# A transposing DMA for the rows of the summed tanh gradient, and one transfer for the rows of F

## The chip, the cores and the metric

The kernel runs on one core of a Trainium2 chip. Its time is the device time of one execution in microseconds, the median of three runs. The profile is of one further execution, taken by the hardware profiler. The engines are TensorE (PE; its weight loads are PEld), VectorE (DVE), ScalarE (ACT), GpSimd (POOL) and SyncE (SP). Each works through its own queue in order. SP computes nothing here: it issues transfers (DMA), as POOL does beside its additions.

## The reference

The kernel computes a small speech model and its gradients. B = 2 sequences of T = 16000 rows with D = 256 features go through two convolutions of three taps, each followed by gelu and a step of 2; the 4000 rows that are left are joined with U = 8 vectors per sequence:

```python
h  = gelu(conv3(x, w1))[:, ::2]          # 8000 rows
f  = gelu(conv3(h, w2))[:, ::2]          # 4000 rows: F
fe = f @ w_f
ge = g @ w_g
j  = tanh(fe[:, :, None, :] + ge[:, None, :, :])
out = j @ w_o                            # (2, 4000, 8, 256)
```

With grad_out given for out, it returns out and the gradients of x, w1, w2, g, w_f, w_g and w_o. One of them matters here. The gradient at fe is the sum over u of (1 - j^2) * (grad_out @ w_o^T); the kernel keeps its negative, bf16, as NGFE. The gradient of w_f is then F^T times that, a product over the 4000 rows of each sequence. TensorE sums over the partitions, so both F and NGFE are needed with rows in the partitions, while the kernel produces both with features in the partitions. The two edits concern how these row forms, FR and NR, are made.

## The kernel before

The two sequences stand behind one another on an axis of 8016 columns, cut into G = 16 chunks of 512 (the last has 336). A tile holds features in the partitions and the columns of a chunk in the free dimension, in KT = 2 halves.

The outer loop runs over the chunks. Pass n has four parts, up = 0 to 3, each with two values of u. A part's main work is the joint of chunk n (joint_units, L670): the gradient of tanh (gj, L612: TensorE multiplies GOT with the transposed w_o at L623, DVE forms NGZ at L627), the sum over u on POOL (ngfe_acc, L632, whose last addition writes NGFE), the output (o_block, L685) and the gradient of w_o (gwo, L721, which reads JR, the rows of the tanh, and GO). weave (L742) alternates it with a fill: after each of the 12 units of main work the fill is due 0.92 units more.

The fill of pass n is the forward convolution of chunk n + 1 and the backward work of chunk n - 1, in a fixed order written at L832: two units of conv, one of d1, one of conv, the other of d1, the last of conv, then rows and d5 in alternation, then gwf, gw2, ghr, conv2 and e. d1 multiplies NGFE with the transposed w_f. row_units (L472) makes the rows: its first unit transposes NGFE by eight TensorE transposes against the identity into one PSUM buffer (L460) and copies it out by one DVE instruction (L462) into a tile of the pool "rows" (six buffers); four more units do the same for h and the gradient behind the second gelu. gwf_units (L499) multiplies FR and NR into the gradient of w_f (L506); it takes 8 matmuls.

The Python order is the order of the work where engines and their data allow it; the framework that builds the program may bring an instruction forward on its engine's queue where its inputs are due earlier, and adds the waits that the tiles need. Every transfer also waits for the one issued eight before it on the same queue kind.

SyncE's queue holds, per pass, eight GOT loads (transposing, L172), four GO loads (plain, L198), eight JR loads (transposing, from JT, L658), four XC loads (transposing, rows of x for chunk n + 2, L164) and the two halves of FR (load_fr, L464, transposing, from FT). JR has two buffers, so the load of one pair of u waits for the gwo matmuls (L729) that read the pair before the last. load_fr(n) stands at the beginning of part up == 1 of pass n; FR has one buffer, and its readers run in pass n + 1.

After the loop a tail does the backward work of chunk 15, and then writes the accumulated gradients; the small gradient of g and w_g uses two small tiles there, gg_sb and ngR.

Of the kernel before, what the change touches and what calls it, by code (L numbers as in the profile page):

```python
# [13 lines left out]
BF16 = mybir.dt.bfloat16  # L14
FP32 = mybir.dt.float32
ALU = mybir.AluOpType
ACT = mybir.ActivationFunctionType
# [5 lines left out]
P = 128  # L23
KT = 2
KK = 3
D = 256
V = 256
U = 8
CW = 512
# [3 lines left out]
def kernel(  # L33
# [22 lines left out]
    nc = tc.nc  # L56
# [7 lines left out]
    def geom(n):  # L64
        c0 = n * CW
        return c0, min(CW, L - c0)

    def segs(n, back=0):

        c0, W = geom(n)  # L70
        out = []
        for b, base in ((0, 0), (1, B1)):
            lo, hi = max(c0 - back, base), min(c0 + W, base + MQ)
            if hi > lo:
# [3 lines left out]
    def gaps(n, back=0):  # L78

        W = geom(n)[1]  # L80
        at, out = -back, []
        for b, q, col, w in segs(n, back):
            if col > at:
                out.append((at, col))
            at = col + w
        if W > at:
            out.append((at, W))
        return out

    def blocks(w):  # L90
        return [(o, min(P, w - o)) for o in range(0, w, P)]

    def nsets(n):
        return 4 if geom(n)[1] == CW else 3

    def sets(n):
        s = nsets(n)
        return [(k, geom(n)[1] // s) for k in range(s)]

    pool = lambda name, bufs, **kw: ctx.enter_context(tc.tile_pool(name=name, bufs=bufs, **kw))  # L100
# [8 lines left out]
    frp = pool("frp", 1)  # L109
    accp = pool("accp", 1)  # L110
    gfp = pool("gfp", 2)
    ghp = pool("ghp", 2)
    rowp = pool("rowp", 6)
    xrp = pool("xrp", 1)
    gxp = pool("gxp", 2)
    jtp = pool("jtp", 7)
# [10 lines left out]
    def ps_f32():  # L127
        return psp.tile([P, 512], FP32, name="ps", tag="ps")

    def ps_bf():  # L130
        return psp.tile([P, 8, P], BF16, name="pst", tag="ps")


    ident = const.tile([P, P], BF16, name="ident")
# [18 lines left out]
    S = [dict() for _ in range(G)]  # L153


    def load_x(n, phases=(0, 1, 3, 2)):
        W = geom(n)[1]
        for c in phases:
            t = xcp.tile([P, KT, CW + 16], BF16, name="XC")
            back = 16 if c == 3 else 0  # L160
            for lo, hi in gaps(n, back):
                nc.vector.memset(t[:, :, 16 + lo:16 + hi], 0.0)
            for b, q, col, w in segs(n, back):
                nc.sync.dma_start_transpose(out=t[:, :, 16 + col:16 + col + w], in_=xq[b, c, q:q + w, :])  # L164
            S[n]["X", c] = t
# [290 lines left out]
    def transposes(srcs, dsts, evict=None):  # L456

        ps = ps_bf()
        for src, j, M in srcs:
            nc.tensor.transpose(out=ps[:M, j, :], in_=src, identity=ident[:])  # L460
        for dst, M, j0, j1 in dsts:
            (evict or nc.vector.tensor_copy)(out=dst, in_=ps[:M, j0:j1, :])  # L462

    def load_fr(n):  # L464
        W = geom(n)[1]
        FR = frp.tile([P, KT, 4, P], BF16, name="FR")
        nb = len(blocks(W))
        for kt in range(KT):
            nc.sync.dma_start_transpose(out=FR[:, kt, 0:nb, :], in_=S[n]["FT"][:, kt, 0:nb * P])
        S[n]["FR"] = FR  # L470

    def row_units(n):  # L472
        c0, W = geom(n)
        st = S[n]
        HT, GF, FT, NG = st["HT"], st["GF"], st["FT"], st["NGFE"]
        bl = blocks(W)
        FR = st["FR"]
        t = rowp.tile([P, 8, P], BF16, name="rows")
        st["NR"] = t
        srcs = [(NG[:, kt, o:o + M], 2 * j + kt, M) for j, (o, M) in enumerate(bl) for kt in range(KT)]  # L480
        dsts = [(t[:M, 2 * j:2 * j + 2, :], M, 2 * j, 2 * j + 2) for j, (o, M) in enumerate(bl)]
        if W == CW:
            dsts = [(t[:], P, 0, 8)]
        transposes(srcs, dsts)
        yield
        st["HG"] = []
        s = nsets(n)
        for k, M in sets(n):
            t = rowp.tile([P, 8, P], BF16, name="rows")
            col = lambda off: slice(off + k, off + k + s * (M - 1) + 1, s)  # L490
            srcs = [(HT[:, par, kt, col(2)], 2 * par + kt, M) for par in range(2) for kt in range(KT)]
            srcs += [(GF[:, kt, col(2)], 4 + kt, M) for kt in range(KT)]
            if k == 0:
                srcs += [(HT[:, 1, kt, col(1)], 6 + kt, M) for kt in range(KT)]
            transposes(srcs, [(t[:M, 0:len(srcs)], M, 0, len(srcs))], nc.scalar.copy)
            st["HG"].append(t)
            yield

    def gwf_units(n):  # L499
        W = geom(n)[1]  # L500
        FR, t = S[n]["FR"], S[n]["NR"]
        bl = blocks(W)
        ps = ps_f32()
        for k, (o, M) in enumerate(bl):
            for dt in range(KT):
                nc.tensor.matmul(ps[:, dt * D:(dt + 1) * D], lhsT=FR[:M, dt, k, :],  # L506
                                 rhs=t[:M, 2 * k:2 * k + 2, :].rearrange("p k d -> p (k d)"),
                                 start=(k == 0 and dt == 0), stop=(k == len(bl) - 1 and dt == KT - 1))
        flush("F", ACCF[:], ps[:])
        first_flush["F"] = False  # L510
        yield
# [226 lines left out]
    def empty(k):  # L738
        for _ in range(k):
            yield  # L740
# [83 lines left out]
    for n in range(G):  # L824
        back, fwd = n > 0, n + 1 < G
        conv = conv_units(n + 1) if fwd else iter(())
        conv2 = conv2_units(n + 1) if fwd else iter(())
        late_open[0] = False
        parts = []
        if back:  # L830
            d1, e, rows, ghr = d1_units(n - 1), e_units(n - 1), row_units(n - 1), ghr_units(n - 1)
            parts += [islice(conv, 2), islice(d1, 1), islice(conv, 1), d1, conv, alternate(rows, d5_units(n - 1)),  # L832
                      gwf_units(n - 1), gw2_units(n - 1), islice(ghr, 1), islice(conv2, 1), ghr, conv2, islice(e, 6)]
            if fwd:
                parts.append(fe_units(n + 1))
            parts.append(e)
        else:
            parts += [conv, empty(3), islice(conv2, 1), empty(3), conv2, empty(3), fe_units(n + 1)]
        fill = chain(*parts)
        ratio = (0.92 if n > 0 else 0.4) if n + 1 < G else 0.72  # L840
        for up in range(U // 2):
            step = n * (U // 2) + up
            for i in range(2):
                if 2 * step + 4 + i < len(order):
                    load_got(*order[2 * step + 4 + i])
            if step + 1 < len(orderp):
                load_go(*orderp[step + 1])
            if up == 1:
                load_fr(n)
            if back and up < 2:  # L850
                load_xr(n - 1, 2 * up)
                load_xr(n - 1, 2 * up + 1)
            main = joint_units(n, up)
            weave(main, fill, ratio)
            if up == U // 2 - 1:
                for _ in fill:
                    pump(2)
                    pump_late(1)
                pump(len(later))
                late_open[0] = True  # L860
                pump_late(len(late))
            for i in range(2):
                if 2 * step + 2 + i < len(order):
                    tanh(*order[2 * step + 2 + i])
            if step + 1 < len(orderp):
                load_jr(*orderp[step + 1])
            if n + 2 < G:
                load_x(n + 2, ((0, 1, 3, 2)[up],))
    n = G - 1
# [9 lines left out]
    for i in range(KK):  # L879
# [15 lines left out]
                            in_=NGGEc[:].rearrange("p b k u c -> p (b k u) c"),  # L895
# [4 lines left out]
    for b in range(B):  # L900
        gg = ps_f32()
        for kt in range(KT):
            nc.tensor.matmul(gg[:U, 0:D], lhsT=NGGEb[:, b, kt, :], rhs=WGT[:, kt, :], start=(kt == 0), stop=(kt == KT - 1))
        gg_sb = gxp.tile([U, D], BF16, name="gg_sb")
        nc.scalar.activation(out=gg_sb[:], in_=gg[:U, 0:D], func=ACT.Copy, scale=-1.0)
        nc.sync.dma_start(out=out_4[b], in_=gg_sb[:])
        tr = ps_bf()
        for kt in range(KT):
            nc.tensor.transpose(out=tr[:U, kt, :], in_=NGGEb[:, b, kt, :], identity=ident[:])
        ngR = gxp.tile([U, KT, P], BF16, name="ngR")  # L910
        nc.vector.tensor_copy(out=ngR[:], in_=tr[:U, 0:KT, :])
        for dt in range(KT):
            nc.tensor.matmul(GWG_ps[:, dt * D:(dt + 1) * D], lhsT=GR8[:, b, dt * P:(dt + 1) * P],
                             rhs=ngR[:].rearrange("u kt p -> u (kt p)"),
                             start=(b == 0 and dt == 0), stop=(b == B - 1 and dt == KT - 1))
# [33 lines left out]
```

## Time and profile before

| what | value |
|---|---|
| median of 3 runs | 849.85 us (844.79 to 854.31) |
| profiled execution | 843.12 us, span 841.4 us |
| granted TensorE clock, mean | 0.994 |
| GOT loads | 136, 5.7 us to landing (median) |
| JR loads | 128, 4.8 us |
| XC loads | 68, 5.6 us |
| FR loads (halves) | 32, 5.6 us |
| mean rate of the transfers | 223 GB/s |

The span runs from the first instruction to the last. "To landing" runs from the start of the issuing instruction to the end of the transfer. In the rows of the profile a name such as `PE ps L524` is an engine, the tile that it writes and a line of the kernel; an arrow to the left in a wait names what ended it. SPq is SyncE's queue; the time of one of its instructions holds any wait in it, and the least that a transposing one takes is about 1.2 us.

### The profile page before, as it was taken

The page shows a single profiled execution, that of the slowest core. Times are in us where ns is not written, and L with a number is a line of the kernel's source. Part 1 is how long each engine was busy: PE and PEld are TensorE (multiplying, and loading weights), DVE is VectorE, ACT ScalarE, POOL GpSimd, SP SyncE. Part 2 cuts the span into 40 slices and gives each one's busy share as a digit, 9 for nine tenths or more (in the row PEclk, how much of TensorE's full clock was granted, in tenths as well). Part 3 has the DMA queues.
Part 4 walks back from the last instruction along what each step waited for, and adds up shares of the span by engine and source line. Part 5 has one row for each costly group of instructions (what it writes and reads, how often), then busy time and mean ns, then how long its engine had stood idle before and what let it go on. Part 6 is the DMA issues. An engine that isn't in the chain of part 4 may idle for free.

```text
span 841.4 us, 17055 instructions
## 1 busy us (share of the span) xinstructions
PE 812.8 (97%) x6396; PEld 598.2 (71%) x6396; DVE 620.3 (74%) x1217; ACT 678.4 (81%) x1080; POOL 394.6 (47%) x423
## 2 busy tenths in 40 slices
PE   7969999999999999999999999999999999999997
PEld 3546677767768677676766777677686776878796
DVE  4896696876778767697866968768687676967644
ACT  3889998796978969699796987969789696987744
POOL 1154544444534535444486644445345354445661
PEclk9999999999999999999999999999999999999999
DMA  9988999999999999999999999999999999999954
GB/s 188 194 198 182 212 229 233 216 251 235 225 221 259 226 229 245 243 222 183 224 255 210 233 233 228 251 210 265 238 237 264 210 227 231 220 210 228 243 157 135
DMA packets 398515, 187.21 MB, mean 223 GB/s; under 512 B 346464, under 2 KB 382200, under 8 KB 398432
## 3 DMA queue, kind: packets, MB, share of 16 engines
q1 hardware_dynamic: 378112, 119.00, 77.9%
q0 software_dynamic: 20320, 67.12, 27.5%
q8 instruction: 50, 0.82, 0.4%
q14 instruction: 33, 0.27, 0.1%
HBM read 51.38 MB, written 50.34 MB: 121 GB/s over the span
## 4 chain that ended last, share of the span: by engine, by line
PE 43%; ACT 41%; DVE 6%; issue 5%; DMA 4%; POOL 0%; SPq 0%; ACTq 0%; POOLq 0%; DVEq 0%
ACT JT L396 12%; PE ps L593 7%; ACT OUT L692 6%; ACT JSQ L617 6%; PE GWO_ps L729 6%; PE ps L580 6%; PE ps L690 6%; ACT rows L462 5%; PE ps L355 5%; PE ps L524 4%; PE ps L623 4%; ACT g_s L260 3%; ACT g_x L323 3%; PE pst L460 2%; ACT GX L583 2%
## 5 line engine op out<-in xcount | busy, mean ns | idle before, releaser
L646 POOL TENSOR_TENSOR ACCN<-ACCN,NGZ 128x1024 f32<-128x1024 f32 (+1 forms) x80 | 168.7, 2109 | 69.1 <-DVE NGZ L627 68.0
L627 DVE SCALAR_TENSOR_TENSOR NGZ<-JSQ,ps 128x512 bf16<-128x512 bf16 (+3 forms) x272 | 167.5, 640 | 43.2 <-PE ps L623 39.9
L692 ACT CAST OUT<-ps 128x512 bf16<-128x512 f32 (+1 forms) x252 | 148.4, 600 | 58.4 <-PE ps L690 58.2
L396 ACT ACTIVATE JT<-FE,GE 128x512 bf16<-128x512 f32 (+3 forms) x272 | 182.3, 711 | 4.0 <-PE ps L623 1.9
L617 ACT ACTIVATE JSQ<-JT 128x1024 bf16<-128x1024 bf16 (+1 forms) x128 | 135.8, 1064 | 25.6 <-DVE NGZ L627 25.6
L729 PE MATMUL GWO_ps<-GO,JR 128*128 128x256 bf16 (+1 forms) x1008 | 148.6, 273 | 2.1 <-DVE JR L462 2.1
L690 PE MATMUL ps<-WO,JT 128*128 128x256 bf16 (+1 forms) x1008 | 148.7, 274 | 0.3 <-ACT rows L462 0.3
L717 POOL DMA_DIRECT2D out_dram<-OUT x76 | 55.8, 735 | 184.4 <-ACT OUT L692 171.5
L623 PE MATMUL ps<-GOT,WOT 128*128 128x512 bf16 (+1 forms) x512 | 139.2, 376 | 0.8 <-DVE rows L462 0.8
L260 DVE SCALAR_TENSOR_TENSOR g_s<-g_sq,g_x 128x1024 bf16<-128x1024 bf16 (+2 forms) x49 | 81.2, 1657 | 50.1 <-ACT g_sq L260 50.1
L729 PEld LDWEIGHTS <-JR 128*128 128x128 bf16 (+1 forms) x1008 | 96.9, 98 | 28.6 <-DVE JR L462 2.4
L690 PEld LDWEIGHTS <-JT 128*128 128x128 bf16 (+1 forms) x1008 | 97.9, 98 | 22.1 <-issue 1.6
L580 PE MATMUL ps<-W1T,GH 128*128 128x256 bf16 (+2 forms) x756 | 100.4, 273 | 0.0
L408 DVE TENSOR_TENSOR ACC<-ACC,ps 128x512 f32<-128x512 f32 x90 | 61.5, 684 | 44.5 <-PE ps L524 32.8
L580 PEld LDWEIGHTS <-GH 128*128 128x128 bf16 (+2 forms) x756 | 83.5, 116 | 13.0
L320 PE MATMUL ps<-XC,W 128*128 128x512 bf16 (+1 forms) x384 | 91.3, 375 | 1.1 <-DMA XC<-in_x_dram 1.1
L593 PE MATMUL ps<-rows,XR 128*128 128x256 bf16 (+1 forms) x756 | 90.4, 273 | 0.0
L593 PEld LDWEIGHTS <-XR 128*128 128x128 bf16 (+1 forms) x756 | 74.0, 98 | 11.6
L583 ACT CAST GX<-ps 128x512 bf16<-128x512 f32 (+2 forms) x126 | 72.2, 587 | 10.5 <-DMA out_dram<-GX 4.1
L241 POOL DMA_DIRECT2D out_dram<-GX x67 | 36.7, 548 | 82.1 <-ACT GX L583 75.0
L623 PEld LDWEIGHTS <-WOT 128*128 128x128 bf16 x512 | 48.5, 98 | 33.6 <-issue 2.3
L320 PEld LDWEIGHTS <-W 128*128 128x128 bf16 x384 | 37.4, 98 | 38.5 <-issue 1.4
(131 smaller groups left out, 1214.2 us busy)
## 6 DMA issues: line engine op xcount, KB each, us to landing
GO<-in_grad_out_dram SPq DMA_DIRECT2D x56, 512.0 KB, 5.3
out_dram<-OUT POOLq DMA_DIRECT2D x56, 512.0 KB, 5.5
out_dram<-GX POOLq DMA_DIRECT2D x55, 256.0 KB, 4.3
XR<-in_x_dram POOLq DMA_DIRECT2D x39, 256.0 KB, 6.3
XR<-in_x_dram POOLq DMA_DIRECT2D x13, 320.0 KB, 6.2
GOT<-in_grad_out_dram SPq DMA_TRANSPOSE x136, 5.7
JR<-JT SPq DMA_TRANSPOSE x128, 4.8
GO<-in_grad_out_dram SPq DMA_DIRECT2D x4, 384.0 KB, 5.0
```

The lines of the kernel that those rows point to most:

```text
L260: later.popleft()()
L320: nc.tensor.matmul(ps[:, :W], lhsT=W1[:, i, kt, mt * P:(mt + 1) * P], rhs=st["X", c][:, kt, 16 + sh:16 + sh + W], start=(k == 0), stop=(k ...
L396: nc.scalar.activation(out=JT[:, mt, lo:hi], in_=S[n]["FE"][:, mt, lo:hi], func=ACT.Tanh, bias=GE[:, b, mt, u:u + 1], scale=1.0)
L580: nc.tensor.matmul(ps[:M, cj * D:(cj + 1) * D], lhsT=GH[:, par, kt, o:o + s * (M - 1) + 1:s], rhs=W1T[:, i, kt, :], start=(j == 0), stop=( ...
L593: nc.tensor.matmul(ps[:, dt * D:(dt + 1) * D], lhsT=XR[:M, 4 * k + i + 2 * (1 - par), dt * P:(dt + 1) * P], rhs=t[:M, g + 2 * par:g + 2 * ...
L617: nc.scalar.activation(out=JSQ[:, :, :W], in_=JT[:, :, :W], func=ACT.Square)
L623: nc.tensor.matmul(ps[:, :W], lhsT=WOT[:, kt, mt * P:(mt + 1) * P], rhs=GOT[:, kt, :W], start=(kt == 0), stop=(kt == KT - 1))
L627: nc.vector.scalar_tensor_tensor(out=NGZ[:, mt, lo:hi], in0=JSQ[:, mt, lo:hi], scalar=1.0, in1=ps[:, lo:hi], op0=ALU.subtract, op1=ALU.mul ...
L646: st["last"] = nc.gpsimd.tensor_tensor(out=out, in0=in0, in1=st["NGZ", u][:, :, :W], op=ALU.add)
L690: nc.tensor.matmul(ps[:M, j * V:(j + 1) * V], lhsT=st["JT", u][:, kt, o:o + M], rhs=WO[:, kt, :], start=(kt == 0), stop=(kt == KT - 1))
L692: nc.scalar.copy(out=OUT[:M, k, :], in_=ps[:M, :])
L729: nc.tensor.matmul(GWO_ps[:, dt, :], lhsT=JR[:M, j, dt, k, :], rhs=GO[:M, k, j * V:(j + 1) * V], start=(n_gwo[0] == 0), stop=(n_gwo[0] == ...
```

## The change

The rows of NGFE get a pool of their own, nrp, with one buffer, and a function load_nr that fills it by a transposing DMA. It is called at the beginning of part up == 1 for chunk n - 1, just ahead of load_fr. row_units makes the rows by TensorE, as before, if NR is not there when it begins; it then copies them in up to four instructions instead of one, as the tile's layout is now [partition, half, block, feature]. FR is loaded by one transfer instead of two for chunks of 512 columns. The two small tiles of the tail are taken from the pool "rows".

```diff
+    nrp = pool("nrp", 1)
...
+    def load_rows(pool_, name, src, W):
+        t = pool_.tile([P, KT, 4, P], BF16, name=name)
+        if W == CW:
+            nc.sync.dma_start_transpose(out=t[:].rearrange("p k a d -> p (k a) d"), in_=src.rearrange("p k w -> p (k w)"))
+        else:
+            nb = len(blocks(W))
+            for kt in range(KT):
+                nc.sync.dma_start_transpose(out=t[:, kt, 0:nb, :], in_=src[:, kt, 0:nb * P])
+        return t
+
     def load_fr(n):
-        W = geom(n)[1]
-        FR = frp.tile([P, KT, 4, P], BF16, name="FR")
-        nb = len(blocks(W))
-        for kt in range(KT):
-            nc.sync.dma_start_transpose(out=FR[:, kt, 0:nb, :], in_=S[n]["FT"][:, kt, 0:nb * P])
-        S[n]["FR"] = FR
+        S[n]["FR"] = load_rows(frp, "FR", S[n]["FT"][:], geom(n)[1])
+
+    def load_nr(n):
+        S[n]["NR"] = load_rows(nrp, "NR", S[n]["NGFE"][:], geom(n)[1])
...
-        t = rowp.tile([P, 8, P], BF16, name="rows")
-        st["NR"] = t
-        srcs = [(NG[:, kt, o:o + M], 2 * j + kt, M) for j, (o, M) in enumerate(bl) for kt in range(KT)]
...
-        transposes(srcs, dsts)
-        yield
+        if "NR" not in st:
+            t = nrp.tile([P, KT, 4, P], BF16, name="NR")
+            st["NR"] = t
+            ps = ps_bf()
+            for j, (o, M) in enumerate(bl):
+                for kt in range(KT):
+                    nc.tensor.transpose(out=ps[:M, 4 * kt + j, :], in_=NG[:, kt, o:o + M], identity=ident[:])
+            for j, (o, M) in enumerate(bl):
+                nc.vector.tensor_copy(out=t[:M, :, j, :], in_=ps[:M, j:j + 5:4, :])
+            yield
...
-                                 rhs=t[:M, 2 * k:2 * k + 2, :].rearrange("p k d -> p (k d)"),
+                                 rhs=t[:M, :, k, :],
...
             if up == 1:
+                if back:
+                    load_nr(n - 1)
                 load_fr(n)
...
-        gg_sb = gxp.tile([U, D], BF16, name="gg_sb")
+        gg_sb = rowp.tile([P, 8, P], BF16, name="rows")[:U, 0:2, :].rearrange("u a b -> u (a b)")
...
-        ngR = gxp.tile([U, KT, P], BF16, name="ngR")
+        ngR = rowp.tile([P, 8, P], BF16, name="rows")[:U, 0:KT, :]
```

More of the change, by code (lines that the diff above doesn't have):

```diff
@@ L477, in row_units @@
         FR = st["FR"]
-        t = rowp.tile([P, 8, P], BF16, name="rows")
-        st["NR"] = t
-        srcs = [(NG[:, kt, o:o + M], 2 * j + kt, M) for j, (o, M) in enumerate(bl) for kt in range(KT)]
-        dsts = [(t[:M, 2 * j:2 * j + 2, :], M, 2 * j, 2 * j + 2) for j, (o, M) in enumerate(bl)]
-        if W == CW:
-            dsts = [(t[:], P, 0, 8)]
-        transposes(srcs, dsts)
-        yield
+        if "NR" not in st:
[8 more added lines that the diff above has]
+            yield
         st["HG"] = []
@@ L903 @@
             nc.tensor.matmul(gg[:U, 0:D], lhsT=NGGEb[:, b, kt, :], rhs=WGT[:, kt, :], start=(kt == 0), stop=(kt == KT - 1))
-        gg_sb = gxp.tile([U, D], BF16, name="gg_sb")
-        nc.scalar.activation(out=gg_sb[:], in_=gg[:U, 0:D], func=ACT.Copy, scale=-1.0)
-        nc.sync.dma_start(out=out_4[b], in_=gg_sb[:])
+        gg_sb = rowp.tile([P, 8, P], BF16, name="rows")[:U, 0:2, :].rearrange("u a b -> u (a b)")
+        nc.scalar.activation(out=gg_sb, in_=gg[:U, 0:D], func=ACT.Copy, scale=-1.0)
+        nc.sync.dma_start(out=out_4[b], in_=gg_sb)
         tr = ps_bf()
@@ L909 @@
             nc.tensor.transpose(out=tr[:U, kt, :], in_=NGGEb[:, b, kt, :], identity=ident[:])
-        ngR = gxp.tile([U, KT, P], BF16, name="ngR")
-        nc.vector.tensor_copy(out=ngR[:], in_=tr[:U, 0:KT, :])
+        ngR = rowp.tile([P, 8, P], BF16, name="rows")[:U, 0:KT, :]
+        nc.vector.tensor_copy(out=ngR, in_=tr[:U, 0:KT, :])
         for dt in range(KT):
```

## The prediction

> **What bounds the kernel now.** The page's first part and the waits of TensorE come first, because they say which engine has no time to give.
>
> ```profile
> PE 812.8 (97%) x6396; PEld 598.2 (71%) x6396; DVE 620.3 (74%) x1217; ACT 678.4 (81%) x1080; POOL 394.6 (47%) x423
> ```
> ```profile
> PE ps L524 <- ACT rows L462: 5.3, 13, 0.7
> PE ps L447 <- DVE GH L450: 3.9, 11, 0.7
> PE ps L320 <- DMA XC<-in_x_dram: 1.1, 1, 1.1
> ```
>
> TensorE is the bound: its largest waits once the loop runs, with total, count and longest, are 5.3 and 3.9 us in all, and the only DMA of a streamed tile that it ever waited for cost 1.1 us. So a wait that is added to TensorE's queue is paid in full. The second question is how far ahead of TensorE the transfers are. The waits of the DMA queue (SyncE) and one outer pass in order of time (n = 5) show it. In the timeline the columns are start, length, engine, line, operation, tiles and count.
>
> ```profile
> SPq L658 <- PE GWO_ps L729: 17.3, 11, 4.8
> JR<-JT SPq DMA_TRANSPOSE x128, 4.8
> ```
> ```profile
> 274.87 2.72 SPq L658 DMA_TRANSPOSE JR<-JT  x2
> ...
> 283.40 0.61 PE L460 MATMUL pst<-ident,NGFE 128*128 128x128 bf16 x8
> ...
> 285.68 0.68 DVE L462 COPY rows<-pst 128x1024 bf16<-128x1024 bf16 x1
> ...
> 288.67 7.90 SPq L164 DMA_TRANSPOSE XC<-in_x_dram  x5
> ...
> 292.66 1.04 PE L506 MATMUL ps<-rows,FR 128*128 128x256 bf16 x8
> ...
> 296.68 3.21 SPq L658 DMA_TRANSPOSE JR<-JT  x2
> ```
>
> The reader should see four things. The rows of NGFE are made by TensorE at 283.4 and copied by 286.4, well before the F-gradient matmuls (L506) at 292.7. SyncE is late in this stretch: the XC loads keep it until 296.6, after L506 has begun. JR takes 4.8 us from issue to landing. And SyncE is tied to TensorE once or twice per pass, where a JR load waits for the GWO matmuls (L729) that free its buffer (first row, 11 visible waits).
>
> **What the change really does to the order.** Per pass the fill advances 0.92 units for each of 12 main units, so 11 units in pass up = 0. Rows begin with the 7th unit (two conv, d1, conv, d1, conv come first). The new load stands at up == 1, later. When row_units asks whether NR exists, it does not, so the TensorE branch runs in every pass; the built order of the changed kernel has the same 6396 matmuls, all 126 transposes of NGFE among them. Then the load comes and replaces NR by a second copy that gwf_units reads. So nothing is removed; a transfer and a wait are added, 15 times (n = 1 to 15; the tail has none).
>
> **Term by term.** All against the profiled execution, 843.1 us (span 841.4 and 1.7 around it; the median of the runs, 849.85, is 0.8% above it).
>
> - Transposes and their copy. 8 transposes started within 0.44 us (the next matmul after 283.40 begins at 283.84), so their removal would have been worth 15 x 0.44 = 6.6 us; it does not happen. The eviction becomes four copies of 128x2x128 for one of 128x1024 (0.688 us). Nearest rows: 0.277 us, the shortest of the tail's copies of 256 columns, and 0.415 us for 128x512. At 0.277 it is 1.11, so +0.42 us on DVE, 6.3 us in all; at 0.415, +0.97 and 14.6. TensorE waits for GH behind this copy, so up to that is at stake; but the place lies ahead of L506, where (below) TensorE waits anyway for something that does not move with it. Cost 0; without that cover 6.
>
> - FR in one transfer: one issue of about 1.3 us in place of two (median 1.42 each); SyncE gains 1.2 us behind the NR slot, and the matmuls that read FR come a whole pass later. 0. The tail's two pairs of small tiles move into rows buffers whose last readers in L524 are done at 825.6, ten us before they are written. 0.
>
> - The new NR load. In the built order SyncE issues it directly ahead of the first JR pair of up = 1, behind all XC loads; the rest of its queue is unchanged. It waits there for the copies of the TensorE branch (done at 286.4 in the pass shown, ten us before SyncE comes by) and for nothing else that is late. What queues behind it are the JR pair, GOT and GO, all with some us to spare. TensorE's L506 now waits for its landing, and behind L506 stands every later matmul.
>
> The price per pass is the start of that JR (the NR slot), plus 4.8 us to land, minus the start of L506. Read from the SyncE and TensorE timelines for n = 1 to 15: 1.6, 5.3, 5.3, 8.3, 8.8, 5.1, 14.0, 9.8, 12.2, 11.2, 9.4, 3.7, 2.9, -1.1, 3.1. For n = 5: 296.68 + 4.8 - 292.66 = 8.8.
>
> Whether this recurs in every pass is the main choice. If SyncE were simply behind, one wait of TensorE would let it catch up for good. But it is tied: in passes 2 to 7 and 13 to 15 a JR load of up = 2 or 3 starts within 1 us of the GWO matmul that frees its buffer. From there SyncE has nine or more issues to make before the NR slot (for n = 6: 324.87 to 343.76, nine issues, 2.1 us each where an undisturbed one takes 1.2), while TensorE needs 18.6 us from the same point to L506. A wait of TensorE moves that starting point with it, so the lateness comes back. Only in passes 8 to 12 is there room: the JR loads lag their GWO matmuls by at least 6.9, 4.6, 6.6, 6.3 and 1.2 us, and by so much SyncE can catch up. Net: 1.6, 5.3, 5.3, 8.3, 8.8, 5.1, 14.0, 2.9, 7.6, 4.6, 3.1, 2.5, 2.9, 0, 3.1: **75 us**. Bounds: if nothing is caught up, 101; if the nine issues ran at 1.25 us, 7.6 us earlier, only n = 4, 5 and 7 would be late, 8 in all. I take 75, because the traffic of that burst does not change.
>
> - The clock. TensorE's waits are paid once more when the granted clock falls. The stretches around its slow spot (window, its length, then busy time and count of PE, PEld, DVE, ACT and POOL, granted clock, share of the DMA engines, GB/s):
>
> ```profile
> 57.00:60.40 3.40, 1.27 (x11) 0.84 (x10) 3.40 (x4) 2.56 (x5) 3.32 (x2) 1.00 0.48 154
> 60.40:63.80 3.40, 1.92 (x8) 0.99 (x7) 3.30 (x5) 1.89 (x3) 0.64 (x1) 0.50 0.48 159
> ```
>
> TensorE was idle for 2.1 of 3.4 us, and the clock stood at 0.50 for the next 6.8 us; eight 128x512 matmuls took 2.83 there, where four take 1.03 at full clock. 13 of the 15 waits exceed 2.1 us. After each, one busy stretch of 3.4 us at half clock loses 1.7 us, two lose 3.4. I take 2.0, near the lower, since one wholly busy stretch (63.8 to 67.2) ended it here: 13 x 2.0 = **26 us**, bounds 0 and 44.
>
> The Trainium skill, "TensorE: Matmul & The Clock Gate", Part 1: The HAM clock gate, puts the fall to half rate behind at least one idle window of about 3.4 us. By that only the waits of over 3.4 us could count, eight of them, which gives 16 us in place of 26 and a time near 929; the two rows speak against it, as a window with 1.27 us of work sufficed.
>
> - What the waits cover: behind L506 stands the wait of L524 for the copied rows (5.3 us in the list above); those copies finish while TensorE waits. **-5**.
>
> Sum: 843.1 + 75 + 26 - 5 = **939 us**, +11% on the profiled execution.
>
> **Rivals.**
>
> - SyncE catches up once. TensorE pays the largest lateness, 14.0, a single time. For it: in passes 8 to 12 SyncE was not tied. Against: the tie in the other ten. To it comes at most the new traffic: the queue's 378112 packets took 77.9% of the span, 1.77 us per 1024 packets of one NR load, 27 us in 15. 857 to 884, about 868.
>
> - The load is hidden, and the time falls. The mechanism: NR no longer holds one of six rows buffers, SyncE is an issue shorter per pass, and if NR lands ahead of L506 only the gain is left: at most the waits on rows, 5.3 and some tenths, so 837. It decides where the NR slot lies 4.8 us ahead of L506. For it: n = 14, where it lay 5.9 ahead. Against: fourteen other passes, by 1.6 to 14 us.
>
> - It does what its words say and the transposes go: 843.1 - 6.6, or 836. The built order excludes it.
>
> **How the numbers follow.** A difference of 1% is about what a measurement of this kernel can tell from none. Forecast (waits in every pass) 0.70, its own range 895 to 985: 50 to 101 of waits, 0 to 44 of clock. Catching up once 0.17. Hidden 0.10, of which 0.04 by more than 1% and 0.06 within it. 0.03 for dearer still. Slower by over 1%: 0.90. The range, 860 to 985, takes in most of the first two and cuts the ends that need all bounds at once.
>
> **What would show it.** The changed profile must have 126 TensorE transposes of NGFE still, 15 NR loads landing in about 5 us, and one new row in TensorE's waits: the matmuls of gwf_units idle behind the DMA of NR for some 75 us in about 14 waits of 2 to 14 us; a granted clock of 0.5 behind most of these waits, and the busy share of TensorE falling in every pass. If the row is there once with about 14 us, the second case holds; if it is missing, the third. I am wrong in size if SyncE's burst ahead of the NR slot gets shorter when TensorE waits, or if half clock lasts longer than one stretch.

## The result, and the profile after

The changed kernel takes 955.0 us (median of 4 runs, 943.2 to 961.8) against 847.3 us before in the same comparison. Two of the four runs, the first profiled one (span 955.9 us) among them, count as slow, being over 1.5% longer than the fastest; the ratio, 1.118 with a 95% interval of 1.101 to 1.135, is that of the other runs. In a later comparison on one chip it was 948.4 against 842.2 us, 1.127 (1.122 to 1.132). A second profile, from there, has a span of 942.9 us and the same shape, and where a size matters both are given.

From the page of the changed kernel, part 1, the clock row of part 2 (40 slices, tenths of full speed) and one group of part 5 (busy, mean ns, idle before it and what ended it):

```profile
PE 841.9 (88%) x6396; PEld 612.2 (64%) x6396; DVE 623.7 (65%) x1262; ACT 678.9 (71%) x1080; POOL 396.0 (41%) x423
...
PEclk9989998979989799798997998979989799999999
...
L517 PE MATMUL ps<-NR,FR 128*128 128x256 bf16 (+1 forms) x126 | 26.4, 380 | 94.6 <-DMA NR<-NGFE 94.6
```

TensorE has the same 6396 matmuls as before and fell from 97% to 88% of a longer span. The matmuls of gwf_units, now L517, stand idle for 94.6 us behind the new load, and nearly every wait leaves a mark in the clock row. The waits of TensorE, total, count and longest, first of this profile and then of the second one:

```profile
PE ps L517 <- DMA NR<-NGFE: 94.6, 14, 10.4
```
```profile
PE ps L517 <- DMA NR<-NGFE: 83.1, 14, 10.0
```

So 94.6 of the 114.5 us by which the span grew is this one wait, and 83.1 of 101.5 in the second profile. The other 20 and 18 us are looked at below. The pass that the prediction showed, n = 5, in order of time (SyncE, then TensorE):

```profile
315.33 8.04 SPq L165 DMA_TRANSPOSE XC<-in_x_dram  x5
323.48 1.25 SPq L468 DMA_TRANSPOSE NR<-NGFE  x1
324.83 2.64 SPq L669 DMA_TRANSPOSE JR<-JT  x2
```
```profile
318.93 0.60 PE L701 MATMUL ps<-WO,JT 128*128 128x256 bf16 x4
326.89 1.87 PE L517 MATMUL ps<-NR,FR 128*128 128x256 bf16 x8 [7.36 <-DMA NR<-NGFE]
```

The XC loads hold SyncE until 323.4, NR is issued at 323.48 and lands 3.3 us later, and TensorE, ready since 319.5, begins at 326.9. That the rows made by TensorE were there long before helps nobody: their tile is replaced. The rows of the NR tile, in the view of that tile, show both copies being made:

```profile
L495 DVE COPY NR<-pst x63: 277/280/286, 80.2 to 935.3; 128x256 bf16<-128x256 bf16 x62, 80x256 bf16<-80x256 bf16 x1
L468 SPq DMA_TRANSPOSE NR<-NGFE x15: 1237/2660/5429, 83.5 to 904.8; - x15
```

### The profile page after: what moved, and what is told of

Its sections match the earlier page's. It is cut to its first block, busy times and chain, and to the rows that moved or that the text cites. A ratio compares the mean times of both kernels' runs of the same rounds, so it can differ in the third digit from the quotient of the medians.

```text
span 955.9 us, 17133 instructions
## 1 busy us (share of the span) xinstructions
PE 841.9 (88%) x6396; PEld 612.2 (64%) x6396; DVE 623.7 (65%) x1262; ACT 678.9 (71%) x1080; POOL 396.0 (41%) x423
## 4 chain that ended last, share of the span: by engine, by line
PE 54%; ACT 21%; DMA 10%; DVE 5%; issue 4%; POOL 3%; SPq 2%; POOLq 0%; ACTq 0%; DVEq 0%
PE GWO_ps L740 8%; DMA NR<-NGFE 8%; PE ps L604 7%; ACT JT L397 7%; PE ps L701 6%; PE ps L591 6%; PE ps L634 6%; PE ps L535 5%; PE ps L356 4%; ACT OUT L703 4%; PE ps L321 3%; ACT JSQ L628 3%; PE ps L517 3%; PE pst L461 2%; SPq L165 2%
## 5 line engine op out<-in xcount | busy, mean ns | idle before, releaser
L703 ACT CAST OUT<-ps 128x512 bf16<-128x512 f32 (+1 forms) x252 | 148.8, 601 | 172.6 <-PE ps L701 172.4
L740 PE MATMUL GWO_ps<-GO,JR 128*128 128x256 bf16 (+1 forms) x1008 | 157.5, 284 | 2.1 <-DVE JR L463 2.1
L634 PE MATMUL ps<-GOT,WOT 128*128 128x512 bf16 (+1 forms) x512 | 139.0, 376 | 2.0 <-DVE GH L451 1.1
L740 PEld LDWEIGHTS <-JR 128*128 128x128 bf16 (+1 forms) x1008 | 101.2, 102 | 32.1 <-DVE JR L463 2.4
L517 PE MATMUL ps<-NR,FR 128*128 128x256 bf16 (+1 forms) x126 | 26.4, 380 | 94.6 <-DMA NR<-NGFE 94.6
L517 PEld LDWEIGHTS <-FR 128*128 128x128 bf16 (+1 forms) x126 | 15.1, 128 | 103.2 <-issue 73.7
L409 DVE TENSOR_TENSOR ACCF<-ACCF,ps 128x512 f32<-128x512 f32 x15 | 10.3, 688 | 107.9 <-PE ps L517 107.8
```

The costliest lines, as they stand in the source:

```text
L634: nc.tensor.matmul(ps[:, :W], lhsT=WOT[:, kt, mt * P:(mt + 1) * P], rhs=GOT[:, kt, :W], start=(kt == 0), stop=(kt == KT - 1))
L703: nc.scalar.copy(out=OUT[:M, k, :], in_=ps[:M, :])
L740: nc.tensor.matmul(GWO_ps[:, dt, :], lhsT=JR[:M, j, dt, k, :], rhs=GO[:M, k, j * V:(j + 1) * V], start=(n_gwo[0] == 0), stop=(n_gwo[0] == ...
```

## The experiments

**Parts of the change by themselves.** First FR in one transfer, on the kernel before:

```diff
-        for kt in range(KT):
-            nc.sync.dma_start_transpose(out=FR[:, kt, 0:nb, :], in_=S[n]["FT"][:, kt, 0:nb * P])
+        if W == CW:
+            nc.sync.dma_start_transpose(out=FR[:].rearrange("p k a d -> p (k a) d"),
+                                        in_=S[n]["FT"][:].rearrange("p k w -> p (k w)"))
```

> The kernel before with FR loaded by one transfer, nothing else changed. Theory (the cost is TensorE's wait for the late NR load): SyncE saves one issue per pass at a place with room, so no change, within 1% of before. Rival (the larger transfer crowds the DMA engines and delays what lies behind it): slower by more than 1%.

Measured: 0.999 of before (0.995 to 1.003). The theory holds; this edit is worth nothing.

Then the changed kernel without the new load, so that the TensorE rows in their new layout are read:

```diff
             if up == 1:
-                if back:
-                    load_nr(n - 1)
                 load_fr(n)
```

> The changed kernel without the call of load_nr, so that the TensorE rows, copied in four instructions, are what the F gradient reads. Theory: within 1% of before, at most 6 us more from 15 x 0.42 us of DVE time, and no wait of TensorE behind a DMA at the F gradient. Rival (the four copies or the new pools hold TensorE up): 870 us or more.

Measured: 1.000 (0.996 to 1.004). The four copies, the new pools and the rows buffers used in the tail cost nothing that shows; the whole loss enters with the call of load_nr.

**The load without its reader, at two sizes.** The load is issued, but the F gradient reads the TensorE rows:

```diff
     def load_nr(n):
-        S[n]["NR"] = load_rows(nrp, "NR", S[n]["NGFE"][:], geom(n)[1])
+        load_rows(nrp, "NR", S[n]["NGFE"][:], geom(n)[1])
...
-            t = nrp.tile([P, KT, 4, P], BF16, name="NR")
+            t = rowp.tile([P, 8, P], BF16, name="rows")[:].rearrange("p (k a) d -> p k a d", k=KT)
```

> The changed kernel with the NR load issued at its place, but its tile never read: the F gradient takes the TensorE rows from a tile of the pool rows. All transfers and all TensorE work of the changed kernel are there; only the wait is gone. Theory: 847 to 860 us, with 15 NR loads landing in about 5 us and no long wait of TensorE. Rival (the 15 extra transfers crowd out others, 1.77 us each): 870 to 875 us or more.

Measured: 863.6 us, 1.019 (1.010 to 1.028); no wait behind NR. That is between the two ranges and nearer to the theory's: the transfer is not free, and it is a sixth of the loss. One thing in the expectation did not come out as written: since the tile no longer waits for the copies of the TensorE branch, the built order brought the load forward on SyncE, ahead of the XC loads. One row of ScalarE's waits has grown; before, the tanh waited 1.6 us in all for a JR load, twice. TensorE has a row behind ScalarE's copies of the output that is not there before:

```profile
ACT JT L397 <- DMA JR<-JT: 14.2, 7, 4.3
```
```profile
PE ps L448 <- ACT OUT L703: 9.7, 5, 3.3
```

The tanh overwrites a JT buffer that a JR load still has to read; JR is issued behind NR now. In time, five of the seven waits of the tanh are followed some 1.2 us later by one of L448 that is about as long (3.2 and 3.3 us, 3.0 and 3.1 us), a sixth by one of the transposes. Is it NR's turn in the queue that delays JR, or its data? The same kernel with a load of 128 columns of one half:

```diff
-        load_rows(nrp, "NR", S[n]["NGFE"][:], geom(n)[1])
+        t = nrp.tile([P, KT, 4, P], BF16, name="NR")
+        nc.sync.dma_start_transpose(out=t[:, 0, 0:1, :], in_=S[n]["NGFE"][:, 0, 0:P])
```

> As the kernel whose NR load nobody reads (1.9% slower than before), but the load has 128 columns of one half instead of 1024: an eighth of the data, at the same place of SyncE's queue, ahead of a JR pair. Leaves out nothing that an output needs. Theory that the data load the DMA engines: nearly all of the 1.9% goes, 845 to 849 us. Rival (the issue slot of some 1.2 us ahead of the JR pair is what costs): 860 us or more.

Measured: 846.9 us, 1.002 (0.998 to 1.005), with this row among the waits of ScalarE:

```profile
ACT JT L397 <- DMA JR<-JT: 7.7, 3, 2.8
```

The same place with an eighth of the data costs nothing measurable, although the issue still takes 1.18 us (median) where the whole load takes 1.31. It is the data that cost the 1.9%, not the issue slot.

**The load earlier, so that the transposes really go.**

```diff
+            if up == 0 and back:
+                load_nr(n - 1)
             if up == 1:
-                if back:
-                    load_nr(n - 1)
                 load_fr(n)
```

> The changed kernel with load_nr(n - 1) called at up == 0, ahead of the rows units, so that the TensorE branch is left out in 15 passes and only the transfer makes NR. In the built order SyncE then issues it ahead of the JR pair at the end of the pass before, ahead of all XC loads. Theory: it lands some 10 us ahead of its reader, TensorE saves 15 x 0.44 us: 833 to 845 us, and 6 transposes of NGFE are left, in the tail. Rival (a transposing load of NR is too slow or too crowded wherever it stands): TensorE waits for it again, 870 us or more.

Measured: 869.2 us, 1.029 (1.023 to 1.035). The first half of the theory holds: L517 is not among TensorE's waits any more, only the tail's transposes are left, and some 80 of the lost 106 us are back. The second half fails: it is slower than before, though not by the rival's mechanism. The largest waits of TensorE, and the one of ScalarE behind a transfer:

```profile
PE GWO_ps L740 <- DMA JR<-JT: 14.0, 10, 2.3
PE ps L701 <- ACT rows L463: 7.2, 1, 7.2
PE pst L461 <- DVE GF L427: 5.3, 9, 1.1
```
```profile
ACT JT L397 <- DMA JR<-JT: 25.8, 13, 9.7
```

JR, which stands behind NR, is late for both its reader and the tanh. The order of TensorE had moved by one fill unit, because the rows units had lost their first step; so the same with an empty step in its place:

```diff
-            yield
+        yield
         st["HG"] = []
```

> The kernel whose NR load stands at up == 0 (2.9% slower than before), with one difference: the rows units keep an empty first step, so that TensorE's order is that of before without the transposes of NGFE. Theory (the cost there is the added transfer ahead of the JR pair, which ScalarE's tanh and the GWO matmuls wait for, not the shift of the fill by one unit): 855 to 868 us. Rival (the shifted order costs): 838 to 850 us.

Measured: 874.5 us, 1.036 (1.031 to 1.042). The shift of the order is not the cause, and the theory was too low by 7 us. ScalarE waited 23.4 us for JR here, and TensorE's largest wait was behind ScalarE's copies, as with the unread load: `PE ps L634 <- ACT OUT L703: 13.7, 6, 3.9`.

**The reader later.** All work of the changed kernel, the load at its place, the F gradient 13 fill units later:

```diff
-                      gwf_units(n - 1), gw2_units(n - 1), islice(ghr, 1), islice(conv2, 1), ghr, conv2, islice(e, 6)]
+                      gw2_units(n - 1), islice(ghr, 1), islice(conv2, 1), ghr, conv2, islice(e, 3),
+                      gwf_units(n - 1), islice(e, 3)]
...
-            if up == 1:
-                if back:
-                    load_nr(n - 1)
+            if up == 1 and back:
+                load_nr(n - 1)
+            if up == 2:
                 load_fr(n)
```

> The changed kernel with all its work and its NR load at the same place of SyncE's queue, but the F gradient moved about 13 fill units (some 16 us) later in the fill, and the FR load one part later so that it does not wait for it. Theory (the cost is the wait for a late slot): the waits of TensorE behind NR go, 94.6 us in the changed kernel, and the clock stays up; what is left is the extra transfer, 850 to 870 us. Rival (the cost is in the work or the traffic, wherever the reader stands): 930 us or more.

Measured: 863.4 us, 1.022 (1.015 to 1.029). The waits behind NR are gone, and 85 us of the 948.4 with them; the rival falls. Most of what is left is not traffic: the largest wait of TensorE is now

```profile
PE ps L535 <- ACT rows L463: 17.6, 14, 1.7
```

against 5.3 us before. The F gradient had stood between the copies of the rows and their first reader, and covered them; its removal from there costs 12.3 of the 16.4 us by which the span is longer than before.

**Both: no transposes, and the load behind a JR pair.** With the late reader, the load was pinned behind the JR pair of up == 1, and the TensorE branch left out in the loop:

```diff
-        if "NR" not in st:
+        if n == G - 1:
...
             if step + 1 < len(orderp):
                 load_jr(*orderp[step + 1])
+            if up == 0 and back:
+                load_nr(n - 1)
```

(the JR loads and this one are kept in program order, and the empty step of the rows units stays).

> No TensorE transposes of NGFE in the loop; the NR load is issued behind the JR pair of up == 1 instead of ahead of it, the F gradient stands 13 fill units later and the FR load one part later. Theory (what is left of the cost after the wait is the data of one more transposing transfer, wherever it stands): 850 to 865 us, less than the 863 of the late reader by some of the 6.6 us that the transposes took. Rival (only the place ahead of a JR pair costs): 835 to 845 us, faster than before.

Measured: 857.8 us, 1.020 (1.015 to 1.025). Within the theory's range, but not by its reason: no wait of ScalarE for JR is left, and TensorE's largest waits are again the rows, with the one wait for NR behind them:

```profile
PE ps L536 <- ACT rows L463: 17.6, 15, 1.5
PE ps L635 <- ACT rows L463: 6.8, 11, 0.9
PE ps L518 <- DMA NR<-NGFE: 3.7, 1, 3.7
```

The place behind JR removes the delay of JR; the late reader costs what it cost in the experiment before. Whether the load behind JR with the reader only as late as needed would beat the kernel before is open; no version here did.

**Why the lateness recurs.** The prediction said that JR's two buffers tie SyncE to TensorE. A third one:

```diff
-    jrp = pool("jrp", 2)
+    jrp = pool("jrp", 3)
...
-    rowp = pool("rowp", 6)
+    rowp = pool("rowp", 5)
```

> The changed kernel with three JR buffers instead of two (and five rows buffers instead of six to make room). JR loads no longer wait for the GWO matmuls of the pair before the last; SyncE is then tied by the GOT and GO buffers, which leave it some 2.5 to 4 us more. Theory (the lateness of the NR slot recurs because SyncE is tied to TensorE): the waits behind NR fall by 2.5 to 4 us each, 905 to 930 us. Rival (SyncE is late because its queue or the DMA engines are full, not because it is tied): no change, about 955 us.

Measured: 966.2 us, 1.141 (1.132 to 1.151); 102.4 us of waits behind NR in 15. Neither side: the time did not fall, so JR's buffers by themselves are not what makes SyncE late. But a queue that is merely full does not explain it either. SyncE's own waits, of the changed kernel and of this one:

```profile
SPq L669 <- PE GWO_ps L740: 102.9, 28, 6.9
```
```profile
SPq L199 <- PE GWO_ps L740: 137.9, 37, 7.2
```

Before, the first of these rows (JR behind GWO) was 17.3 us in 11. SyncE has a hundred microseconds to spare in the changed kernel, and spends them waiting for TensorE. With three JR buffers the same GWO matmuls hold it back through the buffers of GO (L199), of which there are three as well. So the edit did not cut the tie, it moved it; cutting both was not tried. What the tie does to one pass, n = 5, can be read from the second profile of the changed kernel (SyncE, then TensorE):

```profile
288.23 2.64 SPq L669 DMA_TRANSPOSE JR<-JT  x2
...
319.37 1.25 SPq L468 DMA_TRANSPOSE NR<-NGFE  x1
```
```profile
287.56 0.60 PE L740 MATMUL GWO_ps<-GO,JR 128*128 128x256 bf16 x4
...
322.83 1.86 PE L517 MATMUL ps<-NR,FR 128*128 128x256 bf16 x8 [6.37 <-DMA NR<-NGFE]
```

The JR load starts 0.07 us after the GWO matmuls that free its buffer. From there TensorE is ready for L517 after 28.2 us, while SyncE reaches NR after 31.1 us and the data land 3.3 us later. In passes 3 to 12 of both profiles, but for n = 8, such a load starts 28.2 to 28.6 us before TensorE is ready, and SyncE needs 26 to 35 us from it to NR. So each pass starts anew from a matmul: the lateness is not handed on and not worked off. That it would go with the tie is argued from these rows, not shown by taking the tie away.

**The clock.** 30 matmuls of 128x512 into a buffer that nobody reads, directly ahead of the F gradient in passes 3 to 12:

```diff
+        if 3 <= n + 1 <= 12:
+            spare = ps_f32()
+            for _ in range(30):
+                tc.keep_in_program_order(nc.tensor.matmul(spare[:], lhsT=W1[:, 0, 0, 0:P], rhs=W2[:, 0].rearrange("p k d -> p (k d)"),
+                                                          start=True, stop=True))
         ps = ps_f32()
```

> The changed kernel with 30 extra matmuls of 128x512 (6.5 us at full clock) directly ahead of the F gradient in passes 3 to 12, into a PSUM buffer that nobody reads. They fit into the waits of 7.4 to 10.6 us there. Theory (the waits also cost time through the granted clock): the clock falls less, and the time is shorter than the changed kernel's although there is more work, 930 to 945 us. Rival (the clock costs nothing that matters): 955 us or more.

Measured: 935.2 us, 1.107 (1.100 to 1.115), against 955.0 of the changed kernel, but the intervals of the two overlap. So both went once more side by side:

> The changed kernel once more, unaltered, beside the one with extra matmuls: 943 to 962 us, TensorE waiting some 95 us behind NR, mean granted clock 0.94.

> The kernel with 30 extra matmuls ahead of the F gradient in passes 3 to 12 once more, beside the changed kernel. Theory (the waits cost some 20 us through the clock): 10 to 25 us less than the changed kernel on the same chip although it has 65 us of matmuls more. Rival (the clock costs nothing that matters): the same time or more.

Measured: 948.4 us, 1.127 (1.122 to 1.132), for the changed kernel, with the 83.1 us of waits shown above in place of the 95 expected; 939.1 us, 1.114 (1.109 to 1.119), with the extra matmuls. That is 9 us less, clear of the noise and just short of the 10 that the theory asked for. TensorE's wait there:

```profile
PE ps L522 <- DMA NR<-NGFE: 25.3, 8, 7.0
```

Take the waits and the extra matmuls from the span (some 65 us for the latter, an estimate: the 30 of n = 5 take 6.6 us in the trace, the last one's end included) and 932.9 - 25.3 - 65 = 842.6 us is left, 1 us above the span before; take the 83.1 us from the changed kernel's 942.9 and 859.8 is left, 18 us above it. The mean granted clock was 0.982 with the extra matmuls and 0.949 without. Two stretches of the changed kernel's first profile behind the wait of n = 5 (columns as in the prediction) show where they come from:

```profile
326.00:333.00 7.00, 6.11 (x31) 4.45 (x32) 1.37 (x2) 0.00 (x0) 0.00 (x0) 0.53 0.95 196
333.00:345.00 12.00, 12.00 (x100) 9.10 (x98) 7.22 (x13) 6.63 (x10) 5.25 (x4) 1.00 1.01 182
```

For some 6 us after the wait the clock is at half, and the eight matmuls of L517 take the 1.87 us seen above where they took 1.04 before.

## Why the prediction was right

939 us was forecast, 955.0 and 948.4 measured; by ratio 1.114 against 1.118 and 1.127. Step by step:

- *Nothing is removed.* Right: 6396 matmuls, all of NGFE's transposes among them, and 15 loads more. The rival in which the change does what its words say had nothing to stand on.
- *The copy in four and FR in one transfer cost nothing.* Right, each shown alone (1.000 and 0.999). The copies are 0.28 us each, the lower of the two rows named.
- *The wait behind NR in every pass.* Right in place and kind: 14 waits, the first profile's of 0.8 to 10.4 us, and no other large new one. 75 us was forecast, 94.6 and 83.1 measured. The term that failed is the allowance for catching up in passes 8 to 12. It kept 20.7 us there; measured were 42.1 in the first profile and 35.0 in the second. In the changed kernel SyncE waited for GWO in every one of these passes (28 times in all instead of 11, 30 in the second profile), so nothing was left to catch up with. The allowance was also read too large: by the rows of the kernel before, the JR loads ahead of these passes lag by at least 6.1, 4.2, 5.4, 4.3 and 0.9 us, which would have kept 25.4. Over the other passes 54.4 was forecast and 52.5 and 48.1 measured, though singly they differ (14.0 forecast for n = 7, 9.6 and 10.0 measured); that the sum comes so near is in part luck. The waits are so alike because each pass starts from the same point, as above; what sets the 31 us that SyncE needs from there is not settled. Two counts in the prediction are off without changing it: the tie stands in nine passes besides 8 to 12, not ten, and 50 to 101 us of waits with 0 to 44 of clock give 888 to 983, not 895 to 985.
- *The clock, 26 us, and 5 us covered.* About right together: 21 forecast, 20 and 18 measured as what is left of the growth without the waits. Apart, both were a little low. The busy time of TensorE's 6396 matmuls rose from 812.8 to 841.9 us in the first profile, 29.1 in place of 26, so the waits covered some 9 us in place of 5. The covered wait that was named is confirmed: L535 behind the copies fell from 5.3 to 0.2 us; the waits behind GH fell from 3.9 to 1.1. The Trainium skill, "TensorE: Matmul & The Clock Gate", Part 1: The HAM clock gate, asks for an idle window of some 3.4 us before the fall; twelve of the waits were longer than that in each profile, where the forecast had eight. By the prediction's own bound of 2.1 us a thirteenth would count in the first profile, the 2.6 us of n = 1, but the clock stayed at 1.00 behind it. That rule and the rows' bound therefore give nearly the same price here, and this result cannot tell them apart.
- *Catching up once* (868 us) falls by the 14 waits. *Hidden* (837 us) falls with them, and by the version with the load earlier it would not have come to 837 even so: there the load was in time, the transposes gone, and the time 869. What that rival had left out is the price of the data, which the rival of catching up once had put at up to 27 us; measured by itself it is about 16 us (1.9%). The forecast's own sum has no term for it either. In the changed kernel it does not show: the tanh waited there 2.4 us for a JR load, in the second profile 3.1.

## What to carry to other kernels

A transfer that takes work off the bounding engine must be placed by its queue, not by its call: read where it will stand in the issuing queue, what is ahead of it, and when its reader comes. If a helper decides by asking whether a result is already there, look at which of the two runs first, since here the answer was always no and both ways were paid. And where the transfer queue is busy nearly all the time, as here, one more transfer can delay the ones behind it even if nobody waits for it; moving a reader later to hide it can uncover another wait.

## What had not been expected

The fifteen loads cost 1.9% with no reader at all, and 0.2% with an eighth of the data, although TensorE had waited for streamed transfers for only 1.1 us before. The delay went by a way in which TensorE's waits name no transfer: a JR load later, so a tanh later (14 us of waits on ScalarE), so ScalarE's copies of the output later, for which TensorE then waits. And extra work made a kernel faster: 65 us of matmuls that nobody reads, put into waits, took 9 us off the time, with the mean clock at 0.982 instead of 0.949.
